# A channel mix whose output stage goes from eight block products to seven (Strassen's scheme) from the third unit on

## The chip, the cores and the metric

The kernel runs on one core of a Trainium2 chip. A core has a matrix engine (PE in the profile; PEld is its weight load), a vector engine (DVE), a scalar engine (ACT), GpSimd (POOL) and SyncE (SP), which here issues nearly all transfers. Each engine works through its own queue in order; the queues meet through semaphores. The metric is the time of one execution on the device, in microseconds. Lower is better.

## The reference

Inputs are q, k, v of shape (4, 8, 768, 64), eight memory keys and values per head, and the weights of a channel mix. First comes a local attention: chunks of 32 queries look at 16 keys to the left, their own 32, 8 to the right and the 8 memory keys. Its output, reshaped to x of shape (4, 768, 512), goes through the channel mix:

```
x_prev = x shifted by one token (zero at the start of a sequence)
xk = mu_k * x + (1 - mu_k) * x_prev
xr = mu_r * x + (1 - mu_r) * x_prev
k  = max(xk @ w_k, 0)            # w_k: 512 x 1024
v  = (k * k) @ w_v               # w_v: 1024 x 512
r  = sigmoid(xr @ w_r)           # w_r: 512 x 512
out = r * v
```

Everything is in float32. The change concerns the product that gives v.

## The kernel before

**Units.** The 3072 tokens are cut into 12 units of 256 tokens (`UTOK`), each of two tiles of 128 tokens. For each unit the matrix engine runs, by the names that the list in `te_order` uses: `s` (scores of the attention), `t` (transposes of the softmax, two), `a` (attention times values, two), `g` (gate, two blocks of 128 tokens, accumulator `pr`), `h` (hidden layer, four blocks, accumulator `ph`, two slices of 128 hidden columns each) and `v` (output, four blocks, accumulator `pv`: two token tiles, each in two halves over the hidden dimension). Attention runs ahead: while unit u is in its `h` and `v` blocks, `t` and `a` of unit u+1 and `s` of unit u+2 are slipped in between, and `g` of unit u+1 too.

**Precision.** A float32 product is made of three products in the matrix engine's fp32r format. Each operand is split in a high part (a cast to fp32r) and a low part (the operand minus its high part), and high by high, high by low and low by high are added in PSUM. So a block `v` has 4 slices x 3 = 12 matmuls with a moving operand of 512 columns, a block `h` has 2 x 4 x 3 = 24 of 256 columns, a block `g` 12 of 512. Only unit 0 uses plain float32 (`is_whole`), because its weights are not yet split.

**What the other engines do in a unit.** Softmax: maximum, subtraction, sum, reciprocal and normalization on the vector engine, the exponential on the scalar engine. Copies of the transposed softmax into `aTz` and of the attention's output into `xT`. `prep`: the difference of tokens (`df`), two mixtures, and for each its high part `xh` and its low part `xl` (m=1 for the gate, m=0 for the hidden layer). In `channel_mix`, for each of the four `h` blocks: `f_relu`, `f_sq`, the high part `kh` and the low part `kl`; then, for each of the two token tiles, `f_o`, the product with the gate, and a store. The last tile of the last unit is made by `ends`, in two halves of 256 columns.

**The order of work.** Every piece of work is an `Op` with a cost per engine, dependencies, buffers that it takes (`new`) or uses (`use`) and a due time. `Plan.order` sets each engine's queue before the kernel is built: the matrix engine takes its blocks in the order of `te_order`, everything else is placed by earliest start and due time; an operation made with `either` may go to one of several engines. Buffers with one copy per tag make a new owner wait for every user of the old one. Matmuls on zeros (`warm`) fill the matrix engine's idle time until the first block of the hidden layer.

**Weights.** Ten chunks of float64 weights (as 64-bit words) are loaded in the beginning, turned into float32 (`f_abs`, `f_low`, `f_join`) and split (`f_hi`, `f_lo`). Their raw words and the attention's `qk` tiles share five buffers (`big`).

Of the kernel before, what the change touches and what calls it, by code (L numbers as in the profile page):

```python
# [16 lines left out]
P = 128  # L17
# [16 lines left out]
LEAD = "s0.0 s0.1 t0 a0 t1 a1 h0.0.0 h0.0.1 h0.1.0 s1.0 h0.2.0 s1.1 h0.3.0 h0.3.1 h0.3.2 h0.3.3 g0.0 g0.1 t2 t3 v0.0.0 a2 a3 v0.0.1 s2.0 v0.1.0 v0.1.1 h1.0 h1.1 t4 t5 h1.2 a4 a5 h1.3 g1.0 g1.1"  # L34
UTOK = 256
ROWS = [(0, 0, 1), (0, 1, 1), (1, 0, 2), (2, 0, 2), (3, 0, 2)]
# [8 lines left out]
PE_COST = {"s": 1.6, "t": 0.4, "a": 1.05, "g": BLOCK, "h": BLOCK, "v": BLOCK}  # L45
# [34 lines left out]
class Plan:  # L80
# [22 lines left out]
    def place(self, o, free, held):  # L103
        ready = [(d.end, d.eng) for d in o.deps]
        for s in o.new:
            h = held.get(s.tag, [])
            n = self.bufs[s.tag]
# [12 lines left out]
        return best  # L120

# [14 lines left out]
    def turn(self, goal, ease):  # L136
# [9 lines left out]
        while len(done) < len(self.ops):  # L146
            best = None
            for e, q in todo.items():
                for o in q[: 1 if e == "pe" and len(done) < STRICT else LOOK]:
                    p = self.place(o, free, held)  # L150
                    if p is not None:
                        key = (p[1] + max(0.0, o.due - p[1]) * ease, o.due, o.seq)
                        if best is None or key < best[0]:
                            best = (key, o, p)
            _, o, (_, t, eng, cost, port) = best
# [13 lines left out]
def te_order():  # L169
# [3 lines left out]
    for u in range(1, nu):  # L173
# [4 lines left out]
        seq += h[:2] + [("t", a), ("t", b)] + h[2:3] + [("a", a), ("a", b)] + h[3:]  # L178
# [13 lines left out]
def local_attention__then__channel_mix(  # L192
# [56 lines left out]
    def either(late=False, **alts):  # L249
        return [(n, *alts[n]) for n in alts if n != "pool" or late]  # L250
# [10 lines left out]
    o_id = op(("dma", 0.2), lambda: nc.sync.dma_start(id_sb, ident))  # L261
    o_mu = op(("dma", 0.1), lambda: nc.sync.dma_start(mu_sb[:, 0:2], mu))

    def weight(i):
# [3 lines left out]
        def f_load():  # L268
            T["raw", i] = sb("big", [P, 2 * DM], f"raw{i}", I64)
# [29 lines left out]
        def f_lo(e):  # L299
            l = lo[k] = sb(f"w{i - 1}", [P, 2 * DM], f"wl{i}", F32R)  # L300
            e.tensor_sub(l, T["w", id(hi), k], h.bitcast(F32))

        raw, mag, low = Slot("big"), Slot(f"w{i}"), Slot(f"w{i - 1}")
        bufs.setdefault(mag.tag, 1)
        bufs.setdefault(low.tag, 1)
# [4 lines left out]
        hh = op(either(act=(1.02,), dve=(0.62, True)), f_hi, [j], use=[mag])  # L310
        ll = op(either(dve=(1.15, True), pool=(2.5, True)), f_lo, [hh], new=[low], use=[mag])
# [3 lines left out]
        wdone[id(hi), k] = (hh, ll)  # L315
# [19 lines left out]
    def scores(u):  # L335
# [10 lines left out]
        def f_load(t):  # L346
            b, i = qts[t]
            a = T["qk", t] = sb("big", [P, QKW], f"qk{t}")
            nc.sync.dma_start(a, qk[b, i])  # L349
# [80 lines left out]
        qs = [Slot("big") for _ in ts]  # L430
# [6 lines left out]
        prior.update(s=o_s)  # L437
        return done, es
# [104 lines left out]
    def prep(u):  # L543
# [9 lines left out]
        for m in (1, 0):  # L553
            last = m == 0
# [29 lines left out]
    def ends(u, c, ks, o_g, sgs):  # L584
# [4 lines left out]
        os, rows = Slot("o"), slice(t0 + c * P, t0 + (c + 1) * P)  # L589
        deps, use = wdeps(wv_hl, range(FT // 2)), []  # L590
        for k in ks:
            deps += k[:2]
            use += k[2:]
        for z in range(2):
            s, cols = Slot("m"), slice(z * DM // 2, (z + 1) * DM // 2)
            half = slice(z * DM // 4, (z + 1) * DM // 4)

            def f_s2(z=z, half=half):
                p = T["pv", u, c, z] = ps("m", f"pv{u}_{c}_{z}")[:, : DM // 2]
                wh, wl = ([woven(w[f // 2][:, f % 2 * DM : (f % 2 + 1) * DM])[:, half] for f in range(FT)] for w in wv_hl)  # L600
                for f in range(FT):
                    tc_ = slice(f % 2 * UTOK + c * P, f % 2 * UTOK + (c + 1) * P)
                    kh, kl = T["kh", u, f // 2][:, tc_], T["kl", u, f // 2][:, tc_]
                    for n, (x, w) in enumerate(((kh, wh[f]), (kh, wl[f]), (kl, wh[f]))):
                        nc.tensor.matmul(pairs(p), x, w, start=(f + n == 0), stop=(f == FT - 1 and n == 2))  # L605

            def f_o(z=z, cols=cols):
                if z == 0:
                    T["o", u, c] = sb("o", [P, DM], f"o{u}_{c}")
                nc.vector.tensor_mul(T["o", u, c][:, cols], T["pv", u, c, z], T["sg", u][:, c * DM : (c + 1) * DM][:, cols])  # L610

            def f_st(cols=cols):
                nc.sync.dma_start(out[b, rows, cols], T["o", u, c][:, cols])

            dv = due["v", u, c, z]
            o1 = op(("pe", BLOCK), f_s2, deps, new=[s], use=use, due=dv)
            o2 = op(("dve", 0.35), f_o, [o1, o_g[c]], new=[os] * (z == 0), use=[s, sgs] + [os] * z, due=dv + BLOCK + 2)
            op(("dma", 0.5), f_st, [o2], use=[os], due=dv + BLOCK + 6)

    def channel_mix(u):  # L620
# [84 lines left out]
        for f in range(FT // 2):  # L705
# [13 lines left out]
            s, kf, kh, kl = ms[f], Slot("kf"), Slot(f"kh{f}"), Slot(f"kl{f}")  # L719
            bufs.setdefault(kh.tag, 1)  # L720
            bufs.setdefault(kl.tag, 1)
            if is_whole(u, "v"):
                kf = kh

            def f_relu(e, f=f, kf=kf):
                r = T["kf", u, f] = sb(kf.tag, [P, 2 * UTOK], f"kf{u}_{f}")
                if e is nc.scalar:
                    e.activation(r, T["ph", u, f], AF.Relu)  # L728
                else:
                    e.tensor_scalar_max(r, T["ph", u, f], 0.0)  # L730

            def f_sq(e, f=f):
                q = T["kf", u, f]
# [5 lines left out]
            def f_hi(e, f=f):  # L739
                h = T["kh", u, f] = sb(f"kh{f}", [P, 2 * UTOK], f"kh{u}_{f}", F32R)  # L740
                copy(e, h, T["kf", u, f])

            def f_lo(e, f=f):
                l = T["kl", u, f] = sb(f"kl{f}", [P, 2 * UTOK], f"kl{u}_{f}", F32R)
                e.tensor_sub(l, T["kf", u, f], T["kh", u, f].bitcast(F32))  # L745
# [7 lines left out]
            oa = op(either(act=(0.5,), dve=(0.61,)), f_relu, [o1], new=[kf], use=[s], due=dh + BLOCK + 1.5)  # L753
            ob = op(either(u > 2, act=(0.54,), dve=(0.62, True), pool=(1.23, True)), f_sq, [oa], use=[kf])
            if is_whole(u, "v"):
                ks.append((ob, None, kh, kh))
                continue
            o2 = op(either(act=(0.54,), dve=(0.35, True)), f_hi, [ob], new=[kh], use=[kf])
            o3 = op(either(u > 2, dve=(0.62, True), pool=(1.23, True)), f_lo, [o2], new=[kl], use=[kf, kh])
            ks.append((o2, o3, kh, kl))  # L760

        for c in range(QPU):
            if u == NU - 1 and c == QPU - 1:
                ends(u, c, ks, o_g, sgs)
                continue
            s = Slot("m")
            prev = None
            for half in range(2):
                fs = range(FT // 4 * half, FT // 4 * (half + 1))

                def f_s2(c=c, half=half, fs=fs):
# [3 lines left out]
                    if is_whole(u, "v"):  # L775
                        for f in [2 * f2 + i for f2 in fs for i in range(2)]:
                            w = T["w", id(wv_hl[0]), f // 2][:, f % 2 * DM : (f % 2 + 1) * DM]
                            tc_ = slice(f % 2 * UTOK + c * P, f % 2 * UTOK + (c + 1) * P)
                            nc.tensor.matmul(  # L779
                                p, T["kf", u, f // 2][:, tc_], w, start=(f == 0), stop=(f == FT - 1)  # L780
# [3 lines left out]
                    for f2 in fs:  # L784
                        kh, kl = T["kh", u, f2], T["kl", u, f2]
                        for i in range(2):
                            f = 2 * f2 + i
                            tc_ = slice(i * UTOK + c * P, i * UTOK + (c + 1) * P)
# [16 lines left out]
                prev = op(("pe", FULL if is_whole(u, "v") else BLOCK), f_s2, deps, new=[s] if half == 0 else [], use=use + ([s] if half else []), due=dv)  # L805

# [14 lines left out]
    for i in range(len(chunks)):  # L821
        weight(i)
# [6 lines left out]
    for u in range(NU):  # L829
        channel_mix(u)  # L830
    engines = {"act": nc.scalar, "dve": nc.vector, "pool": nc.gpsimd}
# [62 lines left out]
```

## Time and profile before

| | |
|---|---|
| time, median of 3 runs | 398.7 us (398.62 to 399.07) |
| the profiled execution: its time, its span | 398.54 us, 396.8 us |
| matrix engine busy in the span | 391.0 us |
| vector engine busy | 261.4 us |
| scalar engine busy | 190.4 us |
| GpSimd busy | 3.2 us |
| granted clock of the matrix engine | 1.00 |

The span is the time from the first to the last instruction; the execution's own time is 1.74 us longer. "Busy" of the matrix engine counts overlapping matmuls once, so its pace is better read from the starts of successive blocks. In the chain view each row is a start, a duration and the work that filled it, and `x24` counts instructions. In the waits view the columns are the total of the idle time, how often, and the longest. In the view by windows a count in brackets follows each engine's busy time. In the timeline a bracket at the end of a row is the idle time before it and what ended it.

### The profile page before, as it was taken

Reading aid. Unit: us, or ns where it says so; the run is one execution under the profiler, and the core shown is the slowest. Engines: PE = TensorE matmul, PEld = TensorE weight load, DVE = VectorE, ACT = ScalarE, POOL = GpSimd, SP = SyncE. Lnnn points to the kernel's source line nnn. Section 1 sums busy time; section 2 is a strip of 40 time slices with the busy share of each in tenths; the row PEclk is TensorE's granted clock in tenths of the full one; section 3 lists DMA queues with packets and bytes.
Section 4 is the critical chain, followed back from the end, with each engine's and each line's share of the span. In section 5 each row is a group of like instructions: output and inputs, shape, how many; then the busy total and the mean of one; then the engine's idle time right before and its main releaser. Section 6 shows DMA issues by size and latency. Waiting matters only on the chain.

```text
span 396.8 us, 9822 instructions
## 1 busy us (share of the span) xinstructions
PE 391.0 (99%) x4434; PEld 347.1 (87%) x4434; DVE 261.4 (66%) x377; ACT 190.4 (48%) x269; POOL 3.2 (1%) x13
## 2 busy tenths in 40 slices
PE   8899999999999999999999999999999999999996
PEld 6786559989989988988988998998998998998996
DVE  3879999982694595496396297298288378377121
ACT  1759976751443543544435436346255254342250
POOL 2000000000000000000000000000000000000000
PEclk9999999999999999999999999999999999999999
DMA  8999775322341151152052144132130130100101
GB/s 318 417 402 407 285 302 187 107 81 102 120 180 53 52 207 39 36 202 84 28 163 107 52 126 143 53 110 81 53 107 2 55 107 2 55 2 0 55 0 55
DMA packets 13049, 48.93 MB, mean 123 GB/s; under 512 B 1488, under 2 KB 1872, under 8 KB 12496
## 3 DMA queue, kind: packets, MB, share of 16 engines
q1 hardware_dynamic: 13008, 48.31, 33.0%
q8 instruction: 35, 0.57, 0.6%
q14 instruction: 6, 0.05, 0.1%
HBM read 42.01 MB, written 6.29 MB: 122 GB/s over the span
## 4 chain that ended last, share of the span: by engine, by line
PE 95%; DMA 3%; SPq 1%; DVE 0%; issue 0%; POOL 0%
PE ph L713 30%; PE pv L790 28%; PE pr L636 14%; PE px L469 6%; PE s L374 4%; PE ph L685 4%; PE pv L779 4%; DMA mu_sb<-in_mu_dram 3%; PE pt L452 2%; PE pr L628 2%; PE pv L605 1%; SPq L446 0%; SPq L271 0%; SPq L349 0%; POOL mu_sb L512 0%
## 5 line engine op out<-in xcount | busy, mean ns | idle before, releaser
L713 PE MATMUL ph<-xh,wk 128*128 128x256 f32 x352 | 99.0, 281 | 0.0
L713 PE MATMUL ph<-xl,wk 128*128 128x256 f32 x352 | 96.8, 275 | 0.0
L713 PE MATMUL ph<-xh,wl 128*128 128x256 f32 x352 | 96.8, 275 | 0.0
L728 ACT ACTIVATE kf<-ph 128x512 f32<-128x512 f32 x39 | 23.2, 597 | 98.5 <-PE ph L713 97.6
L713 PEld LDWEIGHTS ph<-xh,wk 128*128 128x128 f32 x352 | 67.5, 192 | 1.2 <-issue 0.2
L713 PEld LDWEIGHTS ph<-xl,wk 128*128 128x128 f32 x352 | 67.5, 192 | 0.5 <-issue 0.2
L713 PEld LDWEIGHTS ph<-xh,wl 128*128 128x128 f32 x352 | 67.6, 192 | 0.0
L790 PE MATMUL pv<-wv,kh 128*128 128x512 f32 x168 | 64.5, 384 | 0.0
L790 PE MATMUL pv<-wv,kl 128*128 128x512 f32 x168 | 63.7, 379 | 0.0
L790 PE MATMUL pv<-wl,kh 128*128 128x512 f32 x168 | 63.7, 379 | 0.0
L745 DVE TENSOR_TENSOR kl<-kf,kh 128x512 fp32r<-128x512 f32 x44 | 29.5, 687 | 49.6 <-ACT kh L245 49.6
L812 DVE TENSOR_TENSOR o<-pv,sg 128x512 f32<-128x512 f32 x23 | 15.9, 692 | 33.9 <-PE pv L790 33.9
L790 PEld LDWEIGHTS pv<-wv,kh 128*128 128x128 f32 x168 | 31.8, 189 | 4.8
L790 PEld LDWEIGHTS pv<-wv,kl 128*128 128x128 f32 x168 | 31.8, 189 | 4.5
L790 PEld LDWEIGHTS pv<-wl,kh 128*128 128x128 f32 x168 | 31.8, 189 | 4.0
L636 PE MATMUL pr<-wr,xh 128*128 128x512 f32 x88 | 33.5, 380 | 0.0
L636 PE MATMUL pr<-wl,xh 128*128 128x512 f32 x88 | 33.4, 379 | 0.0
L636 PE MATMUL pr<-wr,xl 128*128 128x512 f32 x88 | 33.4, 379 | 0.0
L245 ACT CAST xh<-df 128x1024 fp32r<-128x1024 f32 x10 | 15.3, 1531 | 33.4 <-DVE df L560 33.4
L469 PEld LDWEIGHTS px<-aTz,vw 128*64 128x64 f32 x768 | 23.5, 138 | 3.3 <-issue 1.3
L469 PE MATMUL px<-aTz,vw 128*64 128x64 f32 x768 | 25.2, 224 | 0.6 <-issue 0.6
L735 ACT ACTIVATE kf<-kf 128x512 f32<-128x512 f32 x38 | 24.0, 631 | 0.8
(72 smaller groups left out, 562.3 us busy)
## 6 DMA issues: line engine op xcount, KB each, us to landing
qk<-in_qk_dram SPq DMA_DIRECT2D x24, 768.0 KB, 5.9
vw<-in_vw_dram SPq DMA_DIRECT2D x24, 512.0 KB, 4.6
out_dram<-o SPq DMA_DIRECT2D x23, 256.0 KB, 2.0
raw<-in_w_k_dram SPq DMA_DIRECT2D x4, 1024.0 KB, 12.9
raw<-in_w_v_dram SPq DMA_DIRECT2D x4, 1024.0 KB, 8.4
raw<-in_w_r_dram SPq DMA_DIRECT2D x2, 1024.0 KB, 8.4
out_dram<-o SPq DMA_DIRECT2D x2, 128.0 KB, 1.7
id_sb<-in_ident_dram SPq DMA_DIRECT2D x1, 64.0 KB, 5.5
```

Of the source, the lines that this page charges most:

```text
L245: e.copy(dst, src)
L374: nc.tensor.matmul(s5[CHUNK * j : CHUNK * (j + 1), h, d - c, r, :], q4[z, r, j, :], k4[z, r, j, :], start=True, stop=True,)
L469: nc.tensor.matmul(p3[64 * h : 64 * h + 64, 2 * g : 2 * g + 2, CHUNK * j : CHUNK * j + CHUNK], v[:, g, h, j, :], a[:, h, g, j, :], start=True,
L636: nc.tensor.matmul(pairs(p), x[:, k, c * P : (c + 1) * P], woven(w), start=(k + n == 0), stop=(k == KT - 1 and n == 2),)
L685: nc.tensor.matmul(p[:, i * UTOK + c * P : i * UTOK + (c + n) * P], T["w", id(wk_hl[0]), k][:, fc], T["xf", u, 0][:, k, z], start=(i + k + ...
L713: nc.tensor.matmul(pairs(p[:, i * UTOK : (i + 1) * UTOK]), w[:, fc], x[:, :, k].rearrange("p t n -> p n t"), start=(k + n == 0), stop=(k = ...
L728: e.activation(r, T["ph", u, f], AF.Relu)
L735: e.activation(q, q, AF.Square)
L745: e.tensor_sub(l, T["kf", u, f], T["kh", u, f].bitcast(F32))
L779: nc.tensor.matmul(p, T["kf", u, f // 2][:, tc_], w, start=(f == 0), stop=(f == FT - 1))
L790: nc.tensor.matmul(pairs(p), x[:, tc_], woven(w), start=(f + n == 0), stop=(f == FT - 1 and n == 2))
L812: nc.vector.tensor_mul(o, p, sg)
```

## The change

From unit 2 on (`FAST = 2`) the output stage cuts the unit's 256 tokens in two halves of 128, the 1024 hidden rows in two halves of 512 and the 512 output columns in two halves of 256. In place of the eight block products of these halves it makes seven products of sums of blocks (the variant of Strassen's scheme with shared sums), numbered 1 to 7 in `products`.

- **Products.** Each has 4 slices x 3 = 12 matmuls with 256 moving columns. The order is 1, 7, then `s` of a later unit and `g` of the next, then 6, 4, 5, 2, 3. Three accumulators are used: x (products 1 and 2), z (7 and 4), y (6, 5 and 3). Products are added into an accumulator after the vector engine has read its value so far: p2 waits for `a0`, p4 for `ac`, p5 for `u2`, p3 for `c22`. The accumulators x and z take the banks of `t` and `a`.
- **Sums of activations.** Four sums of 128x512 (`d1` to `d4`) per unit, and seven pairs of high and low parts in place of four.
- **Outputs.** `a0` is a copy, `ac`, `u2`, `c21`, `c22`, `c12` are additions and `m11`, `m12` products on 128x256, `m2` is a product on 128x512; before there were two products of 128x512.
- **Sums of weights.** `turn_weights` makes once, after unit 1, the sums of blocks of w_v (eight subtractions) and splits them again, in buffers of other chunks of weights, which are no longer needed.
- **Buffers.** `kf` becomes two halves with one copy each; many parts share tags (`kh0`, `kh1`, `w9`, `kf0`); the five `big` buffers get fixed owners, and `qk` tiles from the ninth on alternate between two.
- **Start and order.** The loads of `ident` and `mu` are issued together; `s1.0` is moved ahead of `h0.1.0`; for unit 1 the mixture of the hidden layer is made before that of the gate. In the last two units one gate block each stands between products 7 and 6. `Plan.filler` puts an operation that fits into the gap ahead of a chosen one. GpSimd is no longer among the engines for any work made with `either`. `ends` is gone.

```diff
+FAST = 2
-PE_COST = {"s": 1.6, ...
+PE_COST = {"p": 1.36, "s": 1.6, ...
...
+    def filler(self, o, p, queue, free, held):
+        best = None
+        for x in queue[:LOOK]:
+            y = self.place(x, free, held)
+            if x is not o and y is not None and y[2] == p[2] and y[1] + y[3] <= p[1] + 0.05:
+                key = (x.due, x.seq)
+                if best is None or key < best[0]:
+                    best = (key, x, y)
+        return (o, p) if best is None else best[1:]
...
+        if u >= FAST:
+            v = [("p", u, n) for n in (1, 7, 6, 4, 5, 2, 3)]
+            if u >= nu - 2:
+                g = [("g", nu - 1, u - (nu - 2))]
+            if u == nu - 1:
+                v = v[:5] + [("p", u, 2, 0), ("p", u, 3), ("p", u, 2, 1)]
+            seq += v[:2] + [("s", u + 2, 0)] + g + v[2:]
+            continue
...
-        return [(n, *alts[n]) for n in alts if n != "pool" or late]
+        return [(n, *alts[n]) for n in alts if n != "pool"]
...
-    o_id = op(("dma", 0.2), lambda: nc.sync.dma_start(id_sb, ident))
-    o_mu = op(("dma", 0.1), lambda: nc.sync.dma_start(mu_sb[:, 0:2], mu))
+    def f_small():
+        nc.sync.dma_start(id_sb, ident)
+        nc.sync.dma_start(mu_sb[:, 0:2], mu)
+    o_id = o_mu = op(("dma", 0.3), f_small)
...
+    def turn_weights():
...
+            t1 = op(sub, minus((k, 0), (k, 1), (k, 0)), split[k] + first_v, use=use)
+            t3 = op(sub, minus((k, 1), (k + 2, 1), (k, 1)), [t1], use=use)
+            t2 = op(sub, minus((k + 2, 1), (k + 2, 1), (k, 0)), [t3] + split[k + 2], use=use)
+            t4 = op(sub, minus((k + 2, 0), (k + 2, 0), (k + 2, 1)), [t2], use=use)
...
+            h = op(half, f_t3h, [t3s[k]] + last_v, use=[mags[k]])
+            l = op(sub, f_t3l, [h] + last_v, use=[mags[k], lows[0]])
...
+        turned.update({5: one, 7: three, 4: rest, 6: rest})
...
+    def products(u, ks, o_g, sgs):
...
+        d3 = op(sub, minus(7, 1, 5), sq[:2], new=[st], use=kfs[:1])
+        halves(1, sq[:2])
+        halves(7, [d3])
+        d2 = op(sub, minus(6, 4, 7), sq[2:] + [d3] + list(parts[7]), use=[st, kfs[1]])
+        d1 = op(sub, plus, sq + [d3], use=kfs)
+        halves(5, [d1])
+        halves(6, [d2])
+        halves(4, sq[2:], [*parts[5], *parts[1]])
+        halves(2, sq[2:], [*parts[1], *parts[7]])
+        d4 = op(sub, minus(3, 2, 6), [d2] + list(parts[2]), use=[kfs[1], st])
+        halves(3, [d4])
...
+                for c in cs:
+                    xh, xl = T["ah", u, n][:, c], low(n)[:, c]
+                    wh, wl = weight_of(n, c)
+                    for i, (x, w) in enumerate(((xh, wh), (xh, wl), (xl, wh))):
+                        nc.tensor.matmul(
+                            o, x, w, start=(n in fresh and c + i == 0), stop=(c == cs[-1] and i == 2), skip_group_check=True
+                        )
...
+        p1 = prod(1, [])
+        a0 = op(either(act=(0.36,), dve=(0.36,)), f_a0, [p1], ...)
+        p7 = prod(7, [])
+        ac = op(half, f_ac, [p7, a0], new=os[1:], use=[zs, os[0]])
+        p6 = prod(6, [])
+        u2 = op(half, adds((1, 0), "y", (0, 1)), [p6, a0, ac], use=[ys] + os)
+        p4 = prod(4, [ac, p7])
+        c21 = op(half, adds((1, 0), "z", (1, 0)), [p4, u2], use=[zs, os[1]], due=dq - 2)
+        p5 = prod(5, [u2, p6])
+        c22 = op(half, adds((1, 1), "y", (1, 1)), [p5, ac], use=[ys, os[1]])
+        m2 = op(sub, lambda: nc.vector.tensor_mul(T["o", u, 1], T["o", u, 1], sg(1)), [c21, c22, o_g[1]], ...)
+        op(("dma", 0.75), store(1), [m2], use=[os[1]], due=dq + 2)
+        if last:
+            p2 = prod(2, [p1, a0], range(FT // 4), (0,))
+            p3 = prod(3, [p5, c22])
+            p2 = prod(2, [p2], range(FT // 4, FT // 2), (1,))
+        else:
+            p2 = prod(2, [p1, a0])
+            p3 = prod(3, [p5, c22])
+        m11 = op(half, lambda: nc.vector.tensor_mul(out_part(0, 0), acc("x"), sg(0, 0)), [p2, a0, o_g[0]], ...)
+        c12 = op(half, adds((0, 1), "y", (0, 1)), [p3, u2, ac], use=[ys, os[0]], due=dq)
+        m12 = op(half, lambda: nc.vector.tensor_mul(out_part(0, 1), out_part(0, 1), sg(0, 1)), [c12, o_g[0]], ...)
...
+        if u >= FAST:
+            products(u, ks, o_g, sgs)
+            return
```

More of the change, by code (lines that the diff above doesn't have):

```diff
@@ L154, in turn @@
                             best = (key, o, p)
-            _, o, (_, t, eng, cost, port) = best
+            _, o, p = best
+            if o.rank is None and ease:
+                o, p = self.filler(o, p, todo[o.alts[0][0]], free, held)
+            _, t, eng, cost, port = p
             o.eng, o.start = eng, t
@@ L314, in weight, with split @@
             prior.update(abs=b, join=j)
-        wdone[id(hi), k] = (hh, ll)
+        def split():
+            hh = op(either(act=(1.02,), dve=(0.62, True)), f_hi, [j], use=[mag])
+            deps, new, use = [hh], [low], [mag]
+            if src is w_v:
+                deps.append(whole[id(hi), k // 2 + FT // 4][0])
+                if k % 2:
+                    deps.append(wdone[id(hi), k - 1][1])
+                    new, use = [], [mag, low]
+            ll = op(either(dve=(1.15, True), pool=(2.5, True)), f_lo, deps, new=new, use=use)
+            wdone[id(hi), k] = (hh, ll)
+        return split
     def later(o):
@@ L582, in prep @@
             mix[u, m] = (o_h, o_l, hs, ls)
-    def ends(u, c, ks, o_g, sgs):
-        b, t0 = units[u]
[L589 to L618, printed above, removed]
@@ new lines, in local_attention__then__channel_mix, with quarter, mag, minus @@
+    first_v = []
+    last_v = []
+    turned, turn_use = {}, []
+    def quarter(w, j):
+        return w.rearrange("p (c t n) -> p (c t) n", c=2, t=2)[:, :, j * P : (j + 1) * P]
+    def turn_weights():
+        mags = [whole[id(wv_hl[0]), k][1] for k in range(4)]
+        split = [list(wdone[id(wv_hl[0]), k]) for k in range(4)]
+        t1h, t1l, m2h, m3h, m3l = Slot("w5"), Slot("big2"), Slot("w6"), Slot("w7"), Slot("w8")
+        sub = ("dve", 0.62, True)
+        half = either(act=(0.56,), dve=(0.35, True))
+        def mag(k):
+            return T["w", id(wv_hl[0]), k]
+        def minus(dst, a, b):
+            return lambda: nc.vector.tensor_sub(*(quarter(mag(k), j) for k, j in (dst, a, b)))
+        t3s, t4s, t1s = [], [], []
+        for k in range(2):
+            use = [mags[k], mags[k + 2]]
+            t1 = op(sub, minus((k, 0), (k, 1), (k, 0)), split[k] + first_v, use=use)
+            t3 = op(sub, minus((k, 1), (k + 2, 1), (k, 1)), [t1], use=use)
+            t2 = op(sub, minus((k + 2, 1), (k + 2, 1), (k, 0)), [t3] + split[k + 2], use=use)
+            t4 = op(sub, minus((k + 2, 0), (k + 2, 0), (k + 2, 1)), [t2], use=use)
+            t1s.append(t1)
+            t3s.append(t3)
+            t4s.append(t4)
+        def first(k):
+            return quarter(mag(k), 0).rearrange("p (c t) n -> p t c n", t=2)
+        def f_t1h(k):
+            def go(e):
+                if k == 0:
+                    T["t1h"] = sb("w5", [P, 2, FT // 2, P], "t1h", F32R)
+                copy(e, T["t1h"][:, :, 2 * k : 2 * k + 2], first(k))
+            return go
+        def f_t1l(k):
+            def go():
+                if k == 0:
+                    T["tl"] = sb("big2", [P, 2, 2, FT // 2, P], "tl", F32R)
+                z = slice(2 * k, 2 * k + 2)
+                nc.vector.tensor_sub(T["tl"][:, 0, :, z], first(k), T["t1h"].bitcast(F32)[:, :, z])
+            return go
+        h = l = None
+        one = []
+        for k in range(2):
+            h = op(half, f_t1h(k), [t1s[k], h], new=[t1h] * (k == 0), use=[mags[k]] + [t1h] * k)
+            l = op(sub, f_t1l(k), [h, l, prior["free"]], new=[t1l] * (k == 0), use=[mags[k], t1h] + [t1l] * k)
+            one += [h, l]
+        three = []
+        for k in range(2):
+            def f_t3h(e, k=k):
+                copy(e, quarter(wv_hl[0][k], 1), quarter(mag(k), 1))
+            def f_t3l(k=k):
+                nc.vector.tensor_sub(quarter(wv_hl[1][k], 1), quarter(mag(k), 1), quarter(wv_hl[0][k].bitcast(F32), 1))
+            h = op(half, f_t3h, [t3s[k]] + last_v, use=[mags[k]])
+            l = op(sub, f_t3l, [h] + last_v, use=[mags[k], lows[0]])
+            three += [h, l]
+        def f_mh(k):
+            def go(e):
+                T["mh", k] = sb(f"w{k + 4}", [P, 2 * DM], f"mh{k}", F32R)
+                copy(e, T["mh", k], mag(k))
+            return go
+        def f_ml(k):
+            def go():
+                if k == 2:
+                    T["ml", k] = T["tl"][:, 1].rearrange("p t c n -> p (t c n)")
+                else:
+                    T["ml", k] = sb("w8", [P, 2 * DM], f"ml{k}", F32R)
+                nc.vector.tensor_sub(T["ml", k], mag(k), T["mh", k].bitcast(F32))
+            return go
+        rest = []
+        for k, hs, ls in ((2, m2h, t1l), (3, m3h, m3l)):
+            h = op(either(act=(1.02,), dve=(0.62, True)), f_mh(k), [t4s[k - 2]] + one + three, new=[hs], use=[mags[k]])
+            l = op(("dve", 1.15, True), f_ml(k), [h, l], new=[ls] * (k == 3), use=[mags[k], hs] + [ls] * (k == 2))
+            rest += [h, l]
+        used = [t1h, t1l, m2h, m3h, m3l, lows[0], lows[1]]
+        turned.update({5: one, 7: three, 4: rest, 6: rest})
+        turn_use.extend(used)
+        mags[3].users.extend(rest)
@@ L819, in channel_mix @@
             op(("dma", 0.75), f_st, [o_o], use=[os], due=dv + BLOCK + 6)
-    for i in range(len(chunks)):
-        weight(i)
+    for split in [weight(i) for i in range(len(chunks))]:
+        split()
     for u in range(NU):
```

243 lines of the change are left out of this document (199 added, 44 removed), and 4 rows, old and new, of the table bufs.

## The prediction

> **What bounds the kernel now.** I read the page first: the busy times, then the vector engine's row in 40 slices.
>
> ```profile
> span 396.8 us, 9822 instructions
> PE 391.0 (99%) x4434; PEld 347.1 (87%) x4434; DVE 261.4 (66%) x377; ACT 190.4 (48%) x269; POOL 3.2 (1%) x13
> DVE  3879999982694595496396297298288378377121
> ```
>
> Because a busy matrix engine may still be a slow one, the waits of the matrix engine came second: all that it waits for in the whole run. They add up to 2.5 us, and the two waits for the vector engine's data are 0.2 us each.
>
> ```profile
> PE warm L840 <- DVE zero_sb L234: 1.2, 1, 1.2
> PE px L469 <- issue: 0.6, 1, 0.6
> PE s L374 <- issue: 0.3, 1, 0.3
> PE ph L685 <- DVE xf L533: 0.2, 1, 0.2
> PE pt L452 <- DVE e L408: 0.2, 1, 0.2
> ```
>
> Third, the chain that ended last: its start, one unit from the middle, and its end.
>
> ```profile
> 4.46 11.82 DMA mu_sb<-in_mu_dram
> 16.91 0.36 DVE xf L533
> 17.32 7.48 PE ph L685 x48
> ...
> 219.13 5.36 PE ph L713 x48
> 224.49 0.87 PE pt L452 x8
> 225.37 2.68 PE ph L713 x24
> 228.04 2.02 PE px L469 x64
> 230.06 2.88 PE ph L713 x24
> 232.94 2.59 PE pv L790 x12
> 235.53 1.42 PE s L374 x89
> 236.94 2.79 PE pv L790 x12
> 239.73 5.18 PE pr L636 x24
> 244.91 5.18 PE pv L790 x24
> 250.09 5.36 PE ph L713 x48
> ...
> 383.01 5.18 PE pv L790 x24
> 388.20 5.37 PE pv L605 x48
> ```
>
> From 17.3 us on the chain is the matrix engine's list of blocks without a gap; the unit takes 250.09 - 219.13 = 30.96 us. What counts is therefore the pace of the blocks. A `pv` block of 12 matmuls with 512 columns takes 2.59 us; the 2.79 us behind `s` holds 0.2 us for the change of work and will be paid by whatever follows `s`. The last `pv` row shows the other shape: 48 matmuls of 256 columns in 5.37 us, 111.9 ns each, each with a weight load of its own.
>
> **The products.** Before, a unit's output is 48 matmuls: 2.59 + 2.59 + 5.18 = 10.36 us. After, it is 7 x 12 = 84 matmuls of the other shape: 84 x 111.9 ns = 9.40 us. That is 0.96 us per unit for units 2 to 10, nine times: 8.64 us. The last unit has 5.18 + 5.37 = 10.55 us now, so it gains 1.15 us. Together 9.8 us. Its bound from below is the same row: the same operand types, number of columns and weight load, so I leave it at 9.8.
>
> On the pace the Trainium skill (TensorE: Matmul & The Clock Gate, Back-to-back issue gap) gives columns / 2.4 + 2.5 ns for isolated matmuls. That would be 215.8 and 109.2 ns, 1.2 us per unit and 12 us in all, as an estimate from that page; the 111.9 ns of the row are slower than it for the narrow shape, and the sum goes by the row.
>
> **The vector engine's share.** Rows by shape, and the unit as a whole:
>
> ```profile
> L745 DVE TENSOR_TENSOR kl<-kf,kh 128x512 fp32r<-128x512 f32 x44 | 29.5, 687 | 49.6 <-ACT kh L245 49.6
> L812 DVE TENSOR_TENSOR o<-pv,sg 128x512 f32<-128x512 f32 x23 | 15.9, 692 | 33.9 <-PE pv L790 33.9
> L610 DVE TENSOR_TENSOR o<-pv,sg 128x256 f32<-128x256 f32 x2 | 0.8, 423 | 4.2 <-PE pv L605 4.2
> L387 DVE TENSOR_REDUCE mx<-s 128x16 f32<-128x1024 f32 x11 | 13.4, 1221 | 0.2
> L301 DVE TENSOR_TENSOR wl<-w,wv 128x1024 fp32r<-128x1024 f32 x4 | 4.8, 1212 | 0.0
> ...
> 17.00:41.00 24.00, 23.77 (x233) 17.71 (x231) 21.12 (x30) 19.23 (x28) 0.00 (x0) 1.00 1.02 407
> 41.00:59.00 18.00, 18.00 (x230) 9.63 (x229) 17.11 (x24) 15.62 (x20) 0.00 (x0) 1.00 0.79 292
> 219.13:250.09 30.96, 30.96 (x371) 28.47 (x370) 20.44 (x30) 14.06 (x20) 0.00 (x0) 1.00 0.31 103
> ```
>
> Per unit the change removes four `kl` (2.75 us) and two `o` (1.38 us). It adds seven low parts (7 x 0.687 = 4.81), four sums (2.77), seven operations of 256 columns (`ac`, `u2`, `c21`, `c22`, `m11`, `c12`, `m12`: 7 x 0.423 = 2.96) and `m2` (0.69). Net 7.1 us: 20.4 becomes 27.5 us, in a period of 30.96 - 0.96 = 30.0 us, so 92% where it was 66%. Casts go from four to seven and `a0` comes, mostly on the scalar engine, which has room (14.06 of 30.96 us). Some 3 to 4 us of what the vector engine does in that unit (a relu, a square, two `aTz` copies, two casts) may go to the scalar engine instead; by then it is 23.5 us, 79%. So the extra work costs nothing as long as it is in time; the cover is the matrix engine's own 30 us, and its margin shrinks from 10.5 to between 2.5 and 6.5 us a unit.
>
> **The hand-offs.** Twice a unit a product may start only when the vector engine has read the bank that it adds to: p5 after `u2`, which follows p6, and p3 after `c22`, which follows p5. In between runs one product (p4, p2): 12 x 111.9 ns = 1.34 us. The read takes 0.42 us, so 0.9 us are left for what still runs on the vector engine when the product ends. A 0.69 us sum fits; a softmax piece of 1.22 us is up to 0.3 us late. The other two reads have longer cover: `ac` has `s` and both gate blocks, `a0` nearly everything. No row shows such a hand-off in the steady part; its ends are 0, as the waits of the matrix engine have it now, and the first rival's price below. I am nearer to 0, because most of what can stand in front is 0.69 us long: I put a fifth of the 20 hand-offs at 0.3 us, 1.2 us in all.
>
> **The sums of weights, once.** Eight subtractions and four low parts of 128x512 (12 x 0.69 = 8.3 us) and two low parts of 1.21 us: 10.7 us on the vector engine, due between the end of unit 1 (95.3 us) and p7 and p6 of unit 2 (about 110 and 118 us).
>
> ```profile
> 95.35 0.69 DVE L812 TENSOR_TENSOR o<-pv,sg 128x512 f32<-128x512 f32 x1 [4.13 <-PE pv L790]
> 99.97 0.69 DVE L745 TENSOR_TENSOR kl<-kf,kh 128x512 fp32r<-128x512 f32 x1 [3.93 <-ACT kh L245]
> ```
>
> The two gaps there are 8.1 us of cover, and some of the subtractions may be made from 59 us on, when unit 0 no longer needs the whole weights. I take 0. If the cover is short, 10.7 - 8.1 = 2.6 us are paid once; a gain is excluded, as this work is new.
>
> **Start and end.** The chain shows 11.82 us of waiting for `mu`, which after the change is issued directly behind `ident`. But taking that wait away uncovers little, because the matrix engine still has attention to do:
>
> ```profile
> 15.93 1.15 PE L469 MATMUL px<-aTz,vw 128*64 128x64 f32 x32
> ```
>
> This ends at 17.08 us, 0.24 before the first `ph`. I take 0.2 us, ends 0 and 0.5 us, since the whole beginning is planned anew. `s1.0` only changes place among blocks that follow without a gap: 0. At the end one 0.42 us operation follows the last matmul now, and the stores lie 2.7 us apart. After, p3 ends half a product (0.67 us) before the last part of p2, and `c12`, `m12` and `m11` (3 x 0.42 us) follow with two stores close together: 0.4 us more, ends 0 and 0.9.
>
> **Buffers and queues.** `hi5` takes p1's buffer, `hi3` p7's, low parts 2 and 3 the one of 1 and 7: their owners end one to two gate blocks (2.6 us each) earlier. Transposes of the next unit wait for `m11` and `c21`; two `h` blocks (5.36 us) lie between. A `qk` load now waits for `s` of the unit before, and stores queue behind it on SP; the next `s` is a unit away.
>
> ```profile
> qk<-in_qk_dram SPq DMA_DIRECT2D x24, 768.0 KB, 5.9
> ```
>
> With 5.9 us to landing against 30 us that costs nothing; so does GpSimd's absence from the list of engines (3.2 us in the first page).
>
> **Sum.** 396.8 - 9.8 (products) - 0.2 (start) + 0.4 (end) + 0 (weights) + 1.2 (hand-offs) = 388.4 us of span. The profiled execution took 398.54 us for 396.8 of span, 1.74 more, and the median of the runs, 398.7, is 0.16 above it: 390.3 us.
>
> **Rivals.** First, slower: the hand-offs. If the planner's queue puts a maximum or a subtraction of the softmax and a low part (1.22 + 0.69 us) in front of `u2` and `c22` in every unit, each is 1.91 - 0.92 = 1.0 us late, 2.0 us per unit, 20 us in all: 396.8 - 9.8 + 0.2 + 20 = 407.2 of span, 409 us. It decides against the change from 1.0 us of waiting per unit on, where 9.8 us over ten units are used up. For it: the vector engine is nearly full from the gate's preparation to the end of the products. Against: the order is planned with these dependencies, and `filler` lets only what fits go ahead. The Trainium skill speaks for this rival (Perfetto Trace Analysis, Optimizing Tensor Performance, Matmuls): independent groups should rotate through PSUM banks, so that reading one overlaps the next, and larger matmuls are more efficient than small ones. Here three banks carry seven products, which is where the wait would come from; no run yet shows it.
>
> Second, the vector engine becomes the bound. The two stretches where it was fullest reach (21.12 + 17.11) / 42.0 = 91%. With 27.5 us of work none of which moves to the scalar engine, and 90% filled, a unit lasts 30.55 us, 0.55 more than the matrix engine needs: 5.5 us in place of the 1.2, so 392.7 of span, 394.6 us. Below 89% the unit would be as long as before. Against it speak the 3 to 4 us that can move.
>
> Third, the gate comes too early.
>
> ```profile
> 234.43 1.23 DVE L576 TENSOR_TENSOR xl<-xf,xh 128x1024 fp32r<-128x1024 f32 x1
> ```
>
> `xl` for the gate is ready at 235.66, the gate starts at 239.73: 4.1 us of margin. Between the `h` blocks and the gate lie 2.59 + 2.79 us of `pv` now and 2 x 1.34 us of products after, so 1.4 us remain, and three operations for p1 and p7 stand where two `kl` stood: 0.7 us. Two more sums in front and each gate of eight units is 0.7 us late: 5.6 us more, 395.9 us.
>
> **How the numbers follow.** A measurement here tells about 0.2% (0.8 us) from no change. Forecast, 388.2 to 392.5 us: 0.66; its low end is the sum with no waits and the better ends of start and tail. Better than that: 0.05. The second or third rival, 392.5 to 397.9: 0.17, most of it up to 394.8. Within 0.2%: 0.04. Slower, by the first rival or the second below 89%: 0.08. So faster 0.88, and 388.2 to 394.8 holds the time about 8 times in 10.
>
> **What would show it.** Right: between units 2 and 10 successive `h` blocks start 30.0 us apart, 12 matmuls of a product take 1.34 us, the vector engine is busy 24 to 27.5 us of it, and the matrix engine waits for it under 0.3 us a unit. The first rival shows as matrix engine waits at the products on additions of 256 columns, the second as a vector engine above 90% in each unit and waits spread over all blocks, the third as waits at `pr` on `xl`. Waits once between 105 and 125 us would be the weights. The prediction is wrong if the unit lasts over 30.4 us, or if the narrow matmuls run slower than 112 ns with these operands.

## The result and the profile after

The changed kernel takes 388.99 us (median of 6 runs, 388.36 to 389.43) against 398.66 us of the kernel before (6 runs, 398.51 to 399.27). The ratio is 0.9752, with a 95% interval of 0.9739 to 0.9764: 9.7 us or 2.5% faster. The forecast was 390.3 us in a range of 388.2 to 394.8. The profiled execution took 388.38 us for 386.6 us of span.

The page's first two lines:

```profile
span 386.6 us, 10715 instructions
PE 380.0 (98%) x4768; PEld 350.2 (91%) x4768; DVE 317.6 (82%) x508; ACT 220.4 (57%) x327; POOL 2.8 (1%) x13
```

All waits of the matrix engine (total, times, longest):

```profile
PE warm L1180 <- DVE zero_sb L260: 1.2, 1, 1.2
PE px L526 <- issue: 1.1, 2, 0.6
PE s L429 <- issue: 0.3, 1, 0.3
PE pt L509 <- DVE e L463: 0.2, 1, 0.2
```

None of them lies behind the first blocks. Rows of the chain (start, duration, work): the start of unit 2, one unit from the middle, and the end. The products stand as `acc` with the letter of their accumulator:

```profile
94.70 5.36 PE ph L1028 x48
...
214.59 5.36 PE ph L1028 x48
...
228.39 1.34 PE accx L856 x12
...
232.49 5.38 PE pr L951 x24
237.86 1.34 PE accy L856 x12
239.20 1.34 PE accz L856 x12
240.54 1.34 PE accy L856 x12
241.88 1.34 PE accx L856 x12
243.22 1.34 PE accy L856 x12
244.56 5.36 PE ph L1028 x48
...
381.61 1.35 PE accy L856 x12
...
383.44 0.42 DVE o L928
```

Every product takes 1.34 us, and the 0.2 us behind `s` moved to the gate (5.38). The unit lasts 244.56 - 214.59 = 29.97 us, where it was 30.96. The same stretch by engine: the vector engine is busy 25.25 us of it (84%), the scalar engine 16.41.

```profile
214.59:244.56 29.97, 29.97 (x406) 28.92 (x406) 25.25 (x42) 16.41 (x26) 0.00 (x0) 1.00 0.30 107
```

And the vector engine's timeline around the two hand-offs of that unit. The first `accy,o` is `u2`, `accz,o` is `c21`, the second `accy,o` is `c22`.

```profile
238.18 1.23 DVE L442 TENSOR_REDUCE mx<-s 128x16 f32<-128x1024 f32 x1
239.32 0.41 DVE L898 TENSOR_TENSOR o<-accy,o 128x256 f32<-128x256 f32 x1
239.65 0.68 DVE L801 TENSOR_TENSOR al<-kf,ah 128x512 fp32r<-128x512 f32 x1
240.25 1.33 DVE L633 TENSOR_TENSOR xl<-df,xh 128x1024 fp32r<-128x1024 f32 x1
241.47 0.45 DVE L898 TENSOR_TENSOR o<-accz,o 128x256 f32<-128x256 f32 x1
241.92 0.42 DVE L898 TENSOR_TENSOR o<-accy,o 128x256 f32<-128x256 f32 x1
```

p6 ends at 239.20; `u2` starts 0.12 us later, behind the maximum, and ends at 239.73, 0.81 us before p5 starts. `c22` ends at 242.34, 0.88 us before p3. There is no gap between the two reads.

From unit 2 on to the last matmul the kernel before took 393.57 - 95.31 = 298.26 us, the new one 382.96 - 94.70 = 288.26 us: 10.0 us. The start of unit 2 in the chain of the kernel before:

```profile
95.31 5.36 PE ph L713 x48
```

The rest is small: unit 2 starts 0.6 us earlier in this pair of executions, and from the last matmul to the end of the span it takes 3.64 us for 3.23.

### The profile page after: what moved, and what is told of

Same layout as the page of the kernel before. It is cut to its first block, busy times and chain, and to the rows that moved or that the text cites. A ratio compares the mean times of both kernels' runs of the same rounds, so it can differ in the third digit from the quotient of the medians.

```text
span 386.6 us, 10715 instructions
## 1 busy us (share of the span) xinstructions
PE 380.0 (98%) x4768; PEld 350.2 (91%) x4768; DVE 317.6 (82%) x508; ACT 220.4 (57%) x327; POOL 2.8 (1%) x13
## 4 chain that ended last, share of the span: by engine, by line
PE 96%; DVE 1%; DMA 1%; issue 0%; ACT 0%
PE ph L1028 31%; PE pr L951 15%; PE accy L856 10%; PE accx L856 7%; PE accz L856 7%; PE px L526 6%; PE s L429 4%; PE ph L1000 4%; PE pv L1112 4%; PE pt L509 3%; PE pv L1124 3%; PE pr L943 2%; DMA qk<-in_qk_dram 1%; PE warm L1180 0%; DVE mx L442 0%
## 5 line engine op out<-in xcount | busy, mean ns | idle before, releaser
L1047 ACT ACTIVATE kf<-ph 128x512 f32<-128x512 f32 x47 | 28.0, 597 | 74.4 <-PE ph L1028 74.3
L273 DVE COPY aTz<-pt 64x512 f32<-64x512 f32 x20 | 13.9, 694 | 28.0 <-PE pt L509 18.0
L801 DVE TENSOR_TENSOR al<-kf,ah 128x512 fp32r<-128x512 f32 x50 | 33.5, 684 | 0.4
L453 ACT ACTIVATE e<-e 128x1024 f32<-128x1024 f32 (+1 forms) x13 | 12.9, 992 | 33.6 <-DVE e L447 33.6
L526 PEld LDWEIGHTS px<-aTz,vw 128*64 128x64 f32 x768 | 23.5, 138 | 3.8 <-issue 2.6
L271 ACT CAST ah<-kf 128x512 fp32r<-128x512 f32 x41 | 25.5, 624 | 1.7 <-DVE kf L779 1.1
L1054 ACT ACTIVATE kf<-kf 128x512 f32<-128x512 f32 x40 | 25.3, 633 | 1.3 <-DVE kf L1049 0.4
L856 PE MATMUL accx<-wv,ah 128*128 128x256 f32 x80 | 22.0, 275 | 0.0
L856 PE MATMUL accx<-wl,ah 128*128 128x256 f32 x80 | 22.0, 275 | 0.0
L856 PE MATMUL accx<-wv,al 128*128 128x256 f32 x80 | 22.0, 275 | 0.0
L963 ACT ACTIVATE sg<-pr 128x512 f32<-128x512 f32 x24 | 14.3, 605 | 9.8 <-PE pr L951 9.8
```

Of the source, the lines that this page charges most:

```text
L271: e.copy(dst, src)
L526: nc.tensor.matmul(p3[64 * h : 64 * h + 64, 2 * g : 2 * g + 2, CHUNK * j : CHUNK * j + CHUNK], v[:, g, h, j, :], a[:, h, g, j, :], start=True,
L801: nc.vector.tensor_sub(low(n), place[n](), T["ah", u, n].bitcast(F32))
L856: nc.tensor.matmul(o, x, w, start=(n in fresh and c + i == 0), stop=(c == cs[-1] and i == 2), skip_group_check=True)
L963: nc.scalar.activation(sg, p, AF.Sigmoid)
L1047: e.activation(part(), p, AF.Relu)
```

## Experiments

The theory: the matrix engine's own columns are the whole gain, ten times 0.98 us, and everything that the scheme adds elsewhere is hidden by margins that can be measured. The rivals: a good part of the gain comes from the new order, buffers and beginning; or there is a price on the vector engine or in the hand-offs that the gain already pays. Ratios are to the kernel before, which ran beside them.

**All but the products.** `FAST = 12`, and no sums of weights.

```diff
-FAST = 2
+FAST = 12
...
-        if u == FAST - 1:
+        if u == FAST - 1 < NU - 1:
```

> All of the change except the seven products and the sums of weights: every unit keeps its eight block products, while the new buffers, the fixed load order, the joint load of ident and mu, the filler and the changed lead stay. If the gain is the matrix engine's 0.98 us per unit in ten units, it goes: 398.66 before, less the 0.6 us by which unit 2 started earlier, plus about 0.4 us for the last tile that is no longer cut in two: 398 to 399 us, and successive units 30.95 us apart. If a good part of the gain lies in the new order and buffers: 393 us or less.

Measured: 398.75 us (10 runs), ratio 0.9998 (0.9989 to 1.0008). Taken together, nothing but the products makes the kernel faster. From the first product of the hidden layer to unit 2 this kernel takes 77.53 us where the kernel before takes 77.99, and from the last matmul to the end 3.81 where that one takes 3.23; the two cancel. The units are 30.95 us apart again:

```profile
219.44 5.36 PE ph L1028 x48
250.39 5.36 PE ph L1028 x48
```

**Half the units.** `FAST = 7`.

> Seven products from unit 7 on in place of unit 2. If each unit gains the same 0.98 us by its columns alone, five units lose it: 389.0 + 4.9 = 393.9 us, with units of 30.95 us before unit 7 and 29.97 us from it on. If the gain is made once (start, sums of weights, end), the time stays near 389.

Measured: 394.13 us (393.97 to 394.23), ratio 0.9876 (0.9862 to 0.9891): 5.1 us are lost with five units. The chain shows where the pace changes, between 30.95 and 29.97 us:

```profile
219.38 5.36 PE ph L1028 x48
250.33 5.36 PE ph L1028 x48
280.30 5.36 PE ph L1028 x48
```

The gain goes with the number of units, so it is neither the beginning nor the end.

**A hand-off without cover.** Product 5 directly behind 6.

```diff
-            v = [("p", u, n) for n in (1, 7, 6, 4, 5, 2, 3)]
+            v = [("p", u, n) for n in (1, 7, 6, 5, 4, 2, 3)]
...
-        p4 = prod(4, [ac, p7])
+        p5 = prod(5, [u2, p6])
+        p4 = prod(4, [ac, p7, p5])
...
-        p5 = prod(5, [u2, p6])
...
-            p2 = prod(2, [p1, a0])
+            p2 = prod(2, [p1, a0, p4])
```

> The order of the products is 1, 7, 6, 5, 4, 2, 3, and the dependencies keep it: p5 follows p6 in the same bank with no product between them. If the cover of 1.34 us is what hides the hand-off, each unit now pays the read (0.42 us) and the two semaphores (about 0.1 us together): 0.5 to 0.6 us per unit, 5 to 6 us in all, 394 to 395 us, as a wait of the matrix engine on the addition u2. If a hand-off is expensive in itself (the first rival), over 1 us per unit: above 399. If it costs nothing: 389.

Measured: 397.61 us (397.11 to 397.8), ratio 0.9962 (0.9947 to 0.9977). Nearly the whole gain is gone. A middle unit takes 220.45 - 189.63 = 30.82 us, 0.85 us more and not 0.55. One row of the waits, and rows of the chain:

```profile
PE accy L856 <- DVE o L898: 5.4, 8, 1.2
```

```profile
189.63 5.36 PE ph L1028 x48
...
212.91 1.35 PE accy L856 x12
214.85 1.57 PE accy L856 x12
216.43 1.34 PE accz L856 x12
...
220.45 5.36 PE ph L1028 x48
```

From p6's start to p4's it takes 3.52 us where two products take 2.68. Some 0.6 us are the idle time for the read, as expected. The other 0.23 us stand in p5 itself: the product that starts on an empty matrix engine takes 1.57 us in the chain. A matmul of this shape lasts 0.28 us in the rows, but they follow each other every 0.11 us, so 0.17 us of the last one are no longer covered by a next one; and the first matmul behind the wait lasts 0.35 us. Together that is 0.24 us, called refilling below; why the first lasts longer was not tested. This agrees with the Trainium skill (Perfetto Trace Analysis, Optimizing Tensor Performance, Matmuls), by which independent groups should rotate through banks so that reading one overlaps the next: a product of another bank in between is worth 0.85 us per unit here.

Not all of the 8.6 us by which this kernel is slower than the changed one are this wait. In the profiled executions six middle units account for 5.1 us. Unit 2 alone loses 2.4 us: its chain leaves the matrix engine from 101.4 to 120.8 us and runs through the softmax, the sums of activations and the gate's preparation, which the planner has placed otherwise there.

**Work in front of the hand-offs.** Six clears of a small tile ahead of `u2` and `c22`, unknown to the planner, then two.

```diff
-            return lambda: nc.vector.tensor_add(out_part(*dst), acc(name), out_part(*src))
+            def go():
+                if name == "y" and dst[0] == 1:
+                    for _ in range(6):
+                        nc.vector.memset(zero_sb, 0.0)
+                nc.vector.tensor_add(out_part(*dst), acc(name), out_part(*src))
+
+            return go
```

The second kernel has `range(2)`.

> Six clears of a 128x256 tile (0.27 us each alone, 0.2 to 0.27 back to back) stand on the vector engine in front of u2 and of c22 in each unit, which the planner does not know of. They change no value that is used. In the trace u2 ended 0.8 us and c22 0.9 us before the product that needs it. With 1.2 to 1.6 us in front of each, p5 is 0.4 to 0.8 us late and p3 1.0 to 1.5 us: 1.4 to 2.3 us per unit, 403 to 412 us, slower than the kernel before. If the vector engine has slack wherever the work stands: 389.

Measured with six: 422.79 us (420.67 to 423.0), ratio 1.0583 (1.0555 to 1.0612), 34 us more than the changed kernel and far outside the expectation. The timeline of the vector engine at the two reads of one unit, and from the chain the starts of units 3 and 9:

```profile
221.10 2.23 DVE L901 MEMSET zero_sb<- 128x256 f32 x6
223.25 0.36 DVE L902 TENSOR_TENSOR o<-accy,o 128x256 f32<-128x256 f32 x1
...
225.79 2.23 DVE L901 MEMSET zero_sb<- 128x256 f32 x6
227.94 0.36 DVE L902 TENSOR_TENSOR o<-accy,o 128x256 f32<-128x256 f32 x1
```

```profile
129.18 5.36 PE ph L1034 x48
...
330.67 5.36 PE ph L1034 x48
```

Two things were wrong. Six clears of one tile take 2.15 us: each lasts 0.27 us and starts 0.12 us after the end of the one before, so they are 0.39 us apart. And the margins are not two: as the vector engine has no gap from `u2` to `c22`, what delays `u2` delays `c22` by as much, and the wait at p5 moves p3 by as much as well, so that almost nothing of the second margin is left. 2.15 - 0.81 = 1.34 us at p5. Then from `u2`'s end to `c22`'s end the vector engine needs 228.30 - 223.61 = 4.69 us, and the matrix engine 2.68 and 0.25 of refilling: 1.8 us more at p3, and 0.25 of refilling there too. That is 1.34 + 0.25 + 1.76 + 0.25 = 3.6 us; the six units from 3 to 8 were (330.67 - 129.18) / 6 = 33.58 us apart, 3.6 more than 29.97.

A small part of the 34 us comes through the clock. In unit 10 the matrix engine waits 2.72 us at p3, and the trace has half the clock for 3.41 us from 365.61 us on. Three of the four executions show a mean clock of 0.994 or 0.995 and take 422.66 to 423.0 us; the one with 1.000 takes 420.67. The kernel with two clears was to tell one margin from two:

> As the kernel with six clears, with two: 0.36 us each as measured there, 0.72 us in front of u2 and of c22 in each unit. Theory now: the two hand-offs share one margin, because the vector engine works without a gap from u2 to c22 (2.6 us) while the matrix engine needs 2.68 us from p5's start to p3's. u2 is then still in time (0.72 against 0.8), and c22 is late by 1.44 - 0.9 = 0.55 us: 0.5 to 0.6 us per unit, about 5.5 us, 394 to 395. Rival: each hand-off has its own 0.8 to 0.9 us, then 0.72 us costs nothing: 389 to 390.

Measured: 392.78 us (392.48 to 393.4), ratio 0.9850 (0.9833 to 0.9867). It lies between the two expectations, but the clears do cost time although each pair is shorter than either margin: one shared margin. The chain at the start and at the end of a unit:

```profile
217.05 5.36 PE ph L1034 x48
...
243.32 1.34 DVE xl L633
245.98 1.60 PE accy L856 x12
```

The chain now runs through the vector engine, p3 takes 1.60 us, and this unit lasts from 217.05 to 247.59, 30.54 us, 0.57 more than without clears. Two clears hold up the read behind them by 0.57 us by the timeline, so 2 x 0.57 less 0.88 of margin is 0.26, and refilling is 0.26. The time rose by 3.8 us and not 5.5, because some of the middle units lost less (0.3 us) and the last three together, where the order differs, only 0.6 us.

**More load on the vector engine, known to the planner.** Two pieces of 1.45 us per unit for which nobody waits.

```diff
+        for i in range(2):
+            op(("dve", 1.45), lambda: [nc.vector.memset(zero_sb, 0.0) for _ in range(4)], sq[3:], due=dq + 4)
```

> Two more pieces of 1.45 us (four clears of a 128x256 tile each) on the vector engine in every unit from the third on, known to the planner and with nobody waiting for them. They change no value that is used. The vector engine's load goes from 25.2 to 28.1 us of the 29.97 us unit, 94%, more than the 27.5 us of the prediction. If the planner can place work in the gaps and the matrix engine stays the bound: 389 to 391 us, waits under 0.2 us per unit. If the vector engine is the bound from about 90% on (the second rival): units of 31.2 us, 400 us or more.

Measured: 390.49 us (389.56 to 390.6), ratio 0.9785 (0.9767 to 0.9803). The middle units stay at 29.97 us without a wait, as the row of one shows. Of the rise, 1.1 us in the profiled execution are lost after them, above all in unit 10, where the chain leaves the matrix engine from 346.5 to 359.5 us and four of the clears stand in front of `u2`. Another 1.1 us are lost ahead of unit 2, in a long beginning, of which more below.

```profile
185.70:215.67 29.97, 29.97 (x406) 28.93 (x406) 26.40 (x49) 17.00 (x26) 0.00 (x0) 1.00 0.31 107
```

The row of the chain at which unit 10 comes back to the matrix engine:

```profile
359.47 1.58 PE accy L856 x12
```

The load did not reach the 94% that were expected. The planner moved one copy into `aTz` (0.69 us) to the scalar engine, whose busy time is 17.00 where it was 16.41. The row's 26.40 us of the vector engine and 0.7 us between the clears make 27.1 of 29.97 us, 90% (91% in other middle units), where the changed kernel has 84%. At that load it still isn't the bound; what would happen above it was not tested. About 2.7 us of clears cost nothing in the middle units in places chosen by the planner, where 1.15 us in front of the two reads cost 0.57 us. In unit 10 the planner's own choice put clears in front of a hand-off, and that was paid.

**Without the filler.** `if o.rank is None and ease:` becomes `if False:`.

> The planner without its filler: an operation with an early due time may now leave a gap in front of it, and later work is pushed back. If the margins come from the short critical list alone, nothing changes: 389. If the filler is what keeps the vector engine's backlog small: waits of the matrix engine at p5, p3 or pr of 0.2 to 0.6 us per unit, 391 to 395.

Measured: 390.20 us (389.79 to 390.66), ratio 0.9782 (0.9762 to 0.9801). The loss is not per unit. The middle units stay at 29.97 us; unit 2 alone takes 126.67 - 95.36 = 31.31 us:

```profile
95.36 5.36 PE ph L1028 x48
...
110.73 1.24 DVE xl L633
...
126.67 5.36 PE ph L1028 x48
```

There several sums of weights and their low parts are made between 96 and 104 us, where the changed kernel makes them from 89 us on. The low parts for p1 and p7 come only at 113.7 us (105.0 in the changed kernel), and a block of the gate now stands ahead of p1 and p7. `xl` is ready at 111.97, no later behind the unit's start than in the changed kernel (16.6 us, there 16.7), but the gate block ahead of p1 and p7 waits for it and goes on at 112.01. So the cover for the sums of weights is real but thin: a poorer order of the same work costs 1.3 us once.

**The end.** The second half of p2 after p3, by one dependency (`prod(2, [p2, p3], ...)`).

> Only the end: in the last unit the second half of p2 waits for p3, so that c12 and m12 run beside its 0.67 us of matmuls. In the trace both halves of p2 came first and p3 last, with c12 and m12 behind it (0.90 us from the last matmul to the last product with the gate). Expected: about 0.55 us there, so 0.35 us less, 388.6 us; the interval will hardly tell it, the end of the chain will.

Measured: 388.96 us (388.53 to 389.31), ratio 0.9752 (0.9736 to 0.9767), the same as the changed kernel. One row of the chain, p3, and the last row of the vector engine's timeline:

```profile
381.05 1.53 PE accy L856 x12
```

```profile
383.40 0.42 DVE L926 TENSOR_TENSOR o<-accx,sg 128x256 f32<-128x256 f32 x1
```

It ends at 383.82 us, where the changed kernel's last operation ends at 383.86: `c12` starts 0.4 us earlier, but with `m12` and this `m11` three operations now stand behind p3 in place of two. Besides, only half a product now lies between p5 and p3, so p3 waits for `c22` (it ends at 380.84) and takes 1.53 us, and the last matmul ends at 383.24 in place of 382.96. A miss.

**The beginning.** The runs of one kernel spread by 1 us, and the profiled executions begin in two ways. These three kernels ran beside a repetition of the changed kernel. One matmul call on zeros makes two instructions in the profile, so `n - 1` leaves out two of the ten.

> The changed kernel itself once more, beside the next three: 388.4 to 389.4 us. The executions profiled so far begin in two ways: the ten matmuls on zeros ahead of the first scores take 3.8 to 4.0 us or 4.6 us, and the first product of the hidden layer starts at 17.2 or 18.1 us.

> Two of the ten matmuls on zeros in front of the first scores are left out; nothing else differs. If they are what delays the scores in the longer beginning (1.18 + 4.6 = 5.8 us, while the first load lands at 5.1), eight take at most 3.7 us, the scores start at 5.1 us in every execution, and the longer half of the runs loses 0.6 us: median 388.5, spread under 0.5 us. If the longer beginning has another cause (the clock, the load itself), no change: median 389.0.

> Four of the ten are left out. As with two, 388.5 us, unless the matrix engine's pace in the attention that follows then suffers: the first scores would take over 1.1 us in place of 0.86, and the time would be 389 or more.

> The loads of ident and mu are separate operations again, so that mu may be issued late, as before the change. The predicted gain of this part was 0.2 us (0 to 0.5): 389.0 to 389.4 us, the first product of the hidden layer 0.2 us later. If mu was on the path as the chain of before shows it: 0.5 us or more.

```diff
-                for _ in range(n):
+                for _ in range(n if busy else n - 1):      # n - 2 in the second kernel
```

| | median, us | runs, us | ratio, 95% interval |
|---|---|---|---|
| the changed kernel again | 389.02 | 388.46 to 389.34 | 0.9754 (0.9741 to 0.9767) |
| two matmuls on zeros fewer | 388.46 | 388.34 to 388.63 | 0.9742 (0.9728 to 0.9755) |
| four fewer | 389.34 | 388.77 to 389.60 | 0.9761 (0.9748 to 0.9775) |
| `mu` loaded on its own | 389.05 | 388.86 to 389.32 | 0.9757 (0.9743 to 0.9770) |

The matrix engine's first rows in a long beginning (the kernel with all but the products, same start), then with two and with four matmuls fewer:

```profile
1.18 4.63 PE L1180 MATMUL warm<-zero_sb 128*128 128x256 f32 x10 [1.18 <-DVE zero_sb L260]
5.75 1.13 PE L429 MATMUL s<-qk 64*32 64x64 f32 x64
```

```profile
1.18 3.59 PE L1180 MATMUL warm<-zero_sb 128*128 128x256 f32 x8 [1.18 <-DVE zero_sb L260]
5.11 0.86 PE L429 MATMUL s<-qk 64*32 64x64 f32 x64 [0.33 <-DMA qk<-in_qk_dram]
```

```profile
1.18 2.93 PE L1180 MATMUL warm<-zero_sb 128*128 128x256 f32 x6 [1.18 <-DVE zero_sb L260]
5.09 1.18 PE L429 MATMUL s<-qk 64*32 64x64 f32 x64 [0.98 <-DMA qk<-in_qk_dram]
```

With ten the scores sometimes start 0.6 us after their data landed, behind matmuls on zeros. With eight they wait for the data, and the five runs lie within 0.3 us. With four fewer the matrix engine is still slow when the scores come: 1.18 us for 0.86, and the next six matmuls on zeros take 2.93 us where they took 1.56 with eight. The kernel with eight is the fastest here, 0.5 us below the changed kernel by the medians; the intervals overlap, so the difference rests on the spread and on the rows of one execution. Loading `mu` on its own costs nothing (389.05 against 389.02): from the first scores to the first product of the hidden layer it takes 12.04 us, 12.03 in the repetition. But `mu` landed at 12.44 us in this run and not at 16.28 as in the kernel before, so the run does not bring back the old wait.

## Why the prediction was right, point by point

- **Products, 9.8 us.** Right: 10.0 us measured, 1.34 us per product. Half the units gave about half the gain, none gave none. The scheme drops an eighth of the columns (84 x 256 for 48 x 512), which would be 1.3 us per unit at the pace of the wide matmuls; 0.3 us of it go to the narrow ones, which take 111.7 ns where half a wide one takes 107.9.
- **Hand-offs, 1.2 us.** The term was wrong; it is 0. The step that failed is "I put a fifth of the 20 hand-offs at 0.3 us": behind the maximum of the softmax `u2` starts only 0.12 us after p6's end, and what stands between `u2` and `c22` fits into the time of p4 and p5.
- **0.9 us for each hand-off.** The size is right (0.81 and 0.88), but the picture of two separate margins was not. They are one, and a wait costs 0.25 us of refilling besides. Therefore the first rival was priced too low: its 1.91 us in front of each read was to cost 2.0 us per unit, and 2.15 us cost 3.6.
- **The vector engine, 23.5 to 27.5 us per unit.** Right: 25.25. The second rival did not come, because the load stayed at 84%. The kernel with more load contradicts its 90% only narrowly: 90 to 91% did not lengthen a unit, and a limit above that is not excluded.
- **The gate.** The margin was to be 1.4 us. `xl` ends at 231.12 (229.89 and 1.23 us), the gate starts at 232.49: 1.37. The third rival did not come, but it is the tightest place beside the hand-offs.

```profile
229.89 1.23 DVE L633 TENSOR_TENSOR xl<-xf,xh 128x1024 fp32r<-128x1024 f32 x1
```

- **Sums of weights, 0.** Right, but by the filler; without it 1.3 us, inside the 2.6 that were given for a lost cover. Of the 8.1 us of gaps that were added up, 4.13 end at 95.35 us, so they lie ahead of the stretch that was named; the planner uses them, as sums are made from 89 us on.
- **Start, 0.2 us, and end, 0.4 us.** The end cost 0.41, by another way than argued: the planner made both halves of p2 first, and two operations of 0.42 us stand behind p3. The start gained 0.6 us in the one pair of executions that was profiled; in both, the scores started at 5.1 us. The first product of the hidden layer starts 17.32 - 17.16 = 0.16 us earlier, which is the 0.2 us given to `mu` (the run with `mu` on its own does not test it); the other 0.45 us come in the replanned blocks up to unit 2 and had no term.
- **Sum.** 390.3 forecast, 388.99 measured. In spans it is 388.4 and 386.6: 1.2 us of hand-offs, 0.4 of the start and 0.2 of the products. The miss of the time is smaller, 1.3 us, by luck: the median of the runs is 0.6 us above the profiled execution, which had a short beginning, where 0.16 was taken. The low end of the range, 388.2, is not quite the sum that it is said to be: 390.3 - 1.2 - 0.3 - 0.4 is 388.4.

## What to carry to other kernels

Where the matrix engine runs without a gap, the time that its own rows give for fewer matmul columns is paid out in full, even if the vector engine goes from 66% to 82%, so long as a planner keeps its work off the hand-offs. Judge that by the margins of the few reads that the matrix engine waits for, not by the busy share: about 2.7 us a unit cost nothing in the gaps of the middle units, and 1.15 us ahead of two reads cost two fifths of the gain. Two reads with no gap between them on the reading engine share one margin.

## What was not expected of the hardware

- A product that starts on an empty matrix engine takes 1.53 to 1.60 us in the chain instead of 1.34.
- Clears of one small tile in a row start 0.39 us apart, while one lasts 0.27.
- The matrix engine reaches its full pace at another moment in each execution. The granted clock in the profile's rows shows 1.00 throughout the beginning, because the clock records of the trace start only with the first full clock. That first record begins at 4.05 us in the changed kernel's execution, at 4.45 with eight matmuls on zeros, at 6.68 in the long beginning shown above, and at 10.21 with six (2.93 us of work and 0.98 us of waiting). The matmuls on zeros are 0.43 us apart before these times and 0.22 us after them. The Trainium skill (TensorE: Matmul & The Clock Gate, What's actually happening) puts the release of the clock at about 3.4 us of sustained work in a window that runs freely. The window is borne out: the full clock lasts 378.88, 382.29, 385.71, 389.12 or 392.53 us in all but one of the profiled executions, in steps of 3.41. The amount of work is not the same each time: from the first matmul at 1.18 us the release comes after 2.9 us in the changed kernel and after 5.5 us in the long beginning. So whether eight are always enough is not shown; one of the five executions has a trace.
